# Experts' second product: both halves of the weights side by side in one product of 512 columns, and the two sums of a slot added on GpSimd

## The chip, the cores and the metric

The kernel runs on one core of one Trainium2 chip. The time is the device time of one execution in microseconds. Three runs before the change lie between 5408.88 and 5410.27, median 5409.32.

## The reference

Three layers follow each other over 8 x 3072 = 24576 tokens of 256 values.

```python
attn = np.maximum(z @ z.T / S, 0.0) ** 2      # per batch, S = 3072
x = u * (attn @ v)
e_idx = np.argmax(x @ w_gate, axis=1)         # one of 8 experts for each token
out = np.zeros((N, D))
for e in range(E):
    mask = e_idx == e
    h = np.maximum(x[mask] @ w1[e], 0.0)      # w1[e]: 256 x 1024
    ye = h @ w2[e]                            # w2[e]: 1024 x 256
    out[mask] = gate_w[mask, None] * eom[mask, e, None] * ye
h = out @ w_in                                # 256 x 2048
result = (h / (1.0 + np.exp(-h))) @ w_out     # 2048 x 256
```

The change touches `h @ w2[e]`, the experts' second product.

## The kernel before

To reach the reference's precision every float32 operand is split in two parts that TensorE takes: a high part (`hi`, a copy rounded to the type of the product) and the rest (`lo`). A product is then the sum of three: high with high, low with high and high with low. `split` makes the two parts, the high one on ScalarE (L107) or VectorE (L109), the rest on VectorE as a subtraction of two SBUF operands (L110).

The work goes through three stages: attention, which also sends each token's row to a place in DRAM that belongs to its expert; the experts; the last layer. In the experts' stage the tokens stand in 103 slots of 256 rows (`NSLOT`), each with one expert. A slot is four steps (`NSUB`), each for 256 of the 1024 hidden values, so there are 412 steps k. The instruction streams are written out by hand: each engine runs its instructions in the order in which the loop over k issues them. Step k issues:

- `s1(k+2)`: the first product of step k+2, 12 products of 256 columns (L739), into a bank of PSUM; then ScalarE writes `h`, the high part of the rectified result (L743), and VectorE writes `l`, the rest, from PSUM and `h` (L744);
- `v1(k)`: the second product of step k, 12 products of 256 columns (L760). For each half h of the slot's 256 rows and each i of two blocks of hidden values there are three: `h` with the weights' low part, `l` with the high part, `h` with the high part. All add to one PSUM bank `acc` of 2 x 256 columns, which stays open for the slot's four steps;
- in a slot's first step `x1_prep(t+1)`: VectorE transposes the gathered rows of the next slot (`xt`, L721), ScalarE writes their high part `x1h`, VectorE the rest `x1l`; s1 of the next slot's first step reads them, and is issued two steps later; then `x_gather(t+3)` on GpSimd's queue (L703);
- in a slot's last step `y_store(t)`: ScalarE copies `acc` to `yt` in SBUF (L766), and an indirect DMA from GpSimd's queue sends the rows to DRAM (L767);
- `w_ahead(k)`: splits of coming steps' weights (`w0b` for the first product, five steps ahead, `w1b` for the second, three ahead), ScalarE and VectorE in turn, and gathers of raw weights for a slot two later (L681);
- from step 96 on some instructions of `w_last`, which convert the last layer's weights (L789 to L801, tiles `wraw` and `wt`), mostly on VectorE.

So VectorE's order in a step is l, then xt and x1l in a slot's first step, then w0b, w1b and the conversion; ScalarE's is h, then x1h or yt, then w0b and w1b. PSUM has two pools of four banks, `ps_s` for the first products and `ps_a` for `acc`. `yt` has two buffers in SBUF. The last slot's sums go to `ylast`, and are stored after the last layer has begun.

Of the kernel before, what the change touches and what calls it, by code (L numbers as in the profile page):

```python
# [8 lines left out]
F32 = mybir.dt.float32  # L9
# [4 lines left out]
AF = mybir.ActivationFunctionType  # L14
ALU = mybir.AluOpType
# [11 lines left out]
B, S, D, DQK = 8, 3072, 256, 64  # L27
# [3 lines left out]
P = 128  # L31
# [8 lines left out]
NSLOT = NT // T + E - 1  # L40
# [15 lines left out]
def fused_kernel(ctx: ExitStack, tc: tile.TileContext, uT, v, zT, wg, w1, w2, w_in, w_out, out):  # L56
    nc = tc.nc
    ve, sc, pe, gp_, sy = nc.vector, nc.scalar, nc.tensor, nc.gpsimd, nc.sync
# [9 lines left out]
    ps_a = ctx.enter_context(tc.tile_pool(name="ps_a", bufs=4, space=bass.MemoryType.PSUM))  # L68
# [36 lines left out]
    def split(hi, lo, src, eng="v"):  # L105
        if eng == "a":
            sc.activation(hi, src, AF.Copy)  # L107
        else:
            ve.tensor_copy(hi, src)  # L109
        return ve.tensor_sub(lo, src, hi.bitcast(F32))  # L110

    beat = []
# [449 lines left out]
    for b in range(1, B):  # L562
        first = (b - 1) * NCH * NJ
# [100 lines left out]
    mp = p1.enter_context(tc.tile_pool(name="mp", bufs=2, reuse_waits="tile"))  # L664
# [5 lines left out]
    XG, X1H, X1L, H1, L1, ACC1, WB = {}, {}, {}, {}, {}, {}, {}  # L670
# [3 lines left out]
    def table(idx, t):  # L674
        return idx[0 if t < NEARLY else 1][:, t:t + 1]
# [11 lines left out]
    def w_split(k, which):  # L687
        if k >= NS1:
            return
        t, fp = divmod(k, NSUB)  # L690
        if which == 0:
            src = raw1[t % 2][:, :, fp * 2 * P:(fp + 1) * 2 * P]
        else:
            src = raw2[t % 2][:, 2 * fp:2 * fp + 2, :]
        w = fp_.tile([P, 2, 2, 2 * P], F32R, name=f"w{which}b", tag=f"w{which}b", bufs=4)
        beat.append(split(w[:, 0], w[:, 1], src, "a"))
        WB[which, k] = w

    def x_gather(t):
# [47 lines left out]
    def v1(k):  # L747
        t, fp = divmod(k, NSUB)
        if fp == 0:
            ACC1[t] = ps_a.tile([P, 2, D], F32, name="acc1", tag="acc")  # L750
        acc = ACC1[t]
        hi, lo = H1.pop(k), L1.pop(k)
        wb = WB.pop((1, k))
        for h in range(2):
            for i in range(2):
                first = fp == 0 and i == 0 and h == 0
                ts = slice(h * P, (h + 1) * P)
                fin = fp == NSUB - 1 and i == 1
                for x, hl, end in ((hi, 1, False), (lo, 0, False), (hi, 0, fin)):
                    pe.matmul(acc[:, h, :], x[:, i, ts], wb[:, hl, i, :], start=first, stop=end,  # L760
                              skip_group_check=True)
                    first = False

    def y_store(t):
        yt = mp.tile([P, 2, D], F32, name="yt", tag="yt", bufs=2) if t < NSLOT - 1 else ylast
        sc.activation(yt, ACC1.pop(t), AF.Copy)  # L766
        gp_.indirect_dma_start(  # L767
            y_d[:, :], bass.IndirectOffsetOnAxis(ap=table(xidx, t), axis=0),
            yt.rearrange("p h d -> p (h d)"), None, bounds_check=NSLOT * P - 1, oob_is_err=False,
        )  # L770
# [141 lines left out]
    def w_ahead(k):  # L912

        for which, n in ((0, k + min(4 + k, 6)), (1, k + min(2 + k, 4))):
            while done[which] < n:
                j = done[which]
                w_split(j, which)
                if j % NSUB == NSUB - 1:
                    w_gather(j // NSUB + 2, which)
                done[which] += 1  # L920
# [29 lines left out]
    x1_prep(0)  # L950
    x_gather(3)
    w_split(0, 0)
    w_split(1, 0)
    w_split(0, 1)
    w_split(2, 0)
# [5 lines left out]
    for k in range(NS1):  # L961
        t, fp = divmod(k, NSUB)
# [4 lines left out]
        for f, a in late.get(k, []):  # L967
            if f in ON_PE:
                f(*a)
        v1(k)  # L970
        if fp == 0:
            x1_prep(t + 1)
            if t + 3 >= 4:
                x_gather(t + 3)
        if fp == NSUB - 1 and t < NSLOT - 1:
            y_store(t)
# [22 lines left out]
        if k == 72:  # L999
# [4 lines left out]
            ylast = wr.tile([P, 2, D], F32, name="ylast")  # L1004
# [9 lines left out]
    for k in range(L1K):  # L1014
        h2(k)
    y_store(NSLOT - 1)
    for k in range(L1K, LOOK):
        s2(k)
# [56 lines left out]
```

## Time and profile before

| | us |
|---|---|
| median of three runs | 5409.32 |
| the profiled execution | 5408.52 |
| its span, first to last instruction | 5406.8 |
| TensorE busy | 5350.7 |
| VectorE busy | 4439.7 |
| ScalarE busy | 2985.1 |
| GpSimd busy | 2054.7 |

The experts' stage lies between about 2113 and 3316 us of the span. The mean granted clock of TensorE over the span is 0.998 of full speed. Busy times are unions of an engine's instructions; a matmul's end is modelled, so TensorE's busy time says little of what its pace is, and the distance from one start to the next says more. "Idle before" is the time for which an engine had nothing running ahead of an instruction, and the name behind the arrow is what released it. A DMA that GpSimd issues counts as busy time of GpSimd while its descriptors are written.

### The profile page before, as it was taken

To read this page: it belongs to the slowest core of one execution; us is meant where nothing else is said; L and a number is where in the kernel's file an instruction comes from. 1 tells how busy PE (TensorE), PEld (TensorE's weight loads), DVE (VectorE), ACT (ScalarE), POOL (GpSimd) and SP (SyncE) were. 2 spreads that over 40 slices of the span, in tenths; PEclk is the share of its full clock that TensorE was granted. 3 is DMA by queue.
4 is the path that set the end of the run, shared out by engine and by line. 5 is a ranking of instruction groups with operands and counts; after the bars stand their busy time and mean duration, and the time that the engine had idled before them with its cause. 6 is when DMAs were issued, how large, how long until landed. Compare 5 with 4: busy or idle time off the path is not lost.

```text
span 5406.8 us, 102756 instructions
## 1 busy us (share of the span) xinstructions
PE 5350.7 (99%) x37448; PEld 4789.9 (89%) x37448; DVE 4439.7 (82%) x9831; ACT 2985.1 (55%) x5555; POOL 2054.7 (38%) x1961
## 2 busy tenths in 40 slices
PE   9999999999999998999999999999999999999999
PEld 8888989898989898999999999888888888888887
DVE  8888888888888887888888887777777777777776
ACT  8777777777777776666666664222222222222222
POOL 0444333333333334443333345333333333333331
PEclk9999999999999999999999999999999999999999
DMA  7111111111111101252222221000000000000000
GB/s 271 43 45 43 43 42 48 47 39 46 39 47 39 39 25 67 77 188 92 85 88 88 89 84 38 25 25 25 25 25 24 27 26 24 25 24 25 25 25 21
DMA packets 142428, 287.06 MB, mean 53 GB/s; under 512 B 55904, under 2 KB 55904, under 8 KB 135520
## 3 DMA queue, kind: packets, MB, share of 16 engines
q0 software_dynamic: 95152, 156.97, 9.4%
q1 hardware_dynamic: 46768, 123.51, 6.6%
q8 instruction: 296, 4.85, 0.4%
q14 instruction: 212, 1.74, 0.1%
HBM read 338.44 MB, written 104.33 MB: 82 GB/s over the span
## 4 chain that ended last, share of the span: by engine, by line
PE 77%; DVE 13%; ACT 5%; issue 4%; POOL 0%; DMA 0%; SPq 0%; POOLq 0%; DVEq 0%; ACTq 0%
PE s L877 19%; PE acc L222 14%; PE s L739 10%; PE acc L760 10%; PE acc L901 6%; PE acc L899 6%; PE acc L900 6%; PE sc L222 4%; DVE lo L110 3%; DVE hi L109 2%; ACT r L245 1%; ACT a L250 1%; DVE z L296 1%; DVE l L320 1%; ACT hi L107 1%
## 5 line engine op out<-in xcount | busy, mean ns | idle before, releaser
L463 POOL DMA_INDIRECT x_d<-z,xi x768 | 783.8, 1021 | 1365.3 <-DVE lo L110 919.6
L884 ACT ACTIVATE sg<-s 128x512 f32<-128x512 f32 x768 | 459.3, 598 | 1525.4 <-PE s L877 1523.3
L833 POOL DMA_INDIRECT yg<-y_d,yi x768 | 807.6, 1052 | 1217.7 <-DVE l L110 1147.2
L222 PE MATMUL acc<-hi,vl 64*128 64x512 f32 x4608 | 1236.9, 391 | 7.5 <-DVE z L282 5.3
L222 PE MATMUL acc<-lo,vh 64*128 64x512 f32 x4608 | 1225.9, 388 | 0.6 <-DVE lo L110 0.5
L222 PE MATMUL acc<-hi,vh 64*128 64x512 f32 x4608 | 1223.6, 387 | 0.0
L877 PE MATMUL s<-yh,wi 128*128 128x512 f32 x3072 | 1070.3, 389 | 0.0
L110 DVE TENSOR_TENSOR lo<-a,hi 128x512 fp32r<-128x512 f32 x1152 | 794.7, 690 | 107.3 <-ACT hi L107 77.7
L885 DVE TENSOR_TENSOR sg<-s,sg 128x512 f32<-128x512 f32 x768 | 530.7, 691 | 418.1 <-ACT sg L884 407.2
L250 ACT ACTIVATE a<-r 128x512 f32<-128x512 f32 x1152 | 707.4, 629 | 142.6 <-DVE lo L110 141.8
L222 PEld LDWEIGHTS acc<-hi,vl 64*128 64x128 f32 x4608 | 730.0, 184 | 50.7 <-DVE z L282 9.4
L222 PEld LDWEIGHTS acc<-hi,vh 64*128 64x128 f32 x4608 | 730.2, 184 | 39.1
L222 PEld LDWEIGHTS acc<-lo,vh 64*128 64x128 f32 x4608 | 728.7, 184 | 38.0 <-DVE lo L110 1.6
L245 ACT ACTIVATE r<-sc 128x512 f32<-128x512 f32 x1152 | 622.4, 592 | 211.7 <-PE sc L222 211.3
L877 PEld LDWEIGHTS s<-yh,wi 128*128 128x128 f32 x3072 | 576.6, 188 | 119.6
L739 PE MATMUL s<-x1h,w0b 128*128 128x256 f32 x3296 | 663.6, 284 | 10.3 <-DVE w0b L110 10.3
L760 PE MATMUL acc<-w1b,h 128*128 128x256 f32 x3296 | 660.8, 283 | 0.0
L877 PE MATMUL s<-yl,wi 128*128 128x512 f32 x1536 | 597.6, 389 | 0.0
L901 PE MATMUL acc<-h,wo 128*128 128x512 f32 x1536 | 597.5, 389 | 0.0
L899 PE MATMUL acc<-h,wo 128*128 128x512 f32 x1536 | 597.5, 389 | 0.0
L900 PE MATMUL acc<-l,wo 128*128 128x512 f32 x1536 | 597.5, 389 | 0.0
L739 PEld LDWEIGHTS s<-x1h,w0b 128*128 128x128 f32 x3296 | 545.0, 192 | 10.9 <-DVE w0b L110 10.0
(210 smaller groups left out, 10443.4 us busy)
## 6 DMA issues: line engine op xcount, KB each, us to landing
x_d<-zero SPq DMA_DIRECT2D x25, 1024.0 KB, 12.5
vr<-in_v_dram SPq DMA_DIRECT2D x48, 512.0 KB, 4.5
ut<-in_uT_dram SPq DMA_DIRECT2D x48, 512.0 KB, 3.6
out_dram<-ot SPq DMA_DIRECT2D x48, 512.0 KB, 2.6
zz<-in_zT_dram SPq DMA_DIRECT2D x96, 128.0 KB, 5.0
x_d<-z,xi POOLq DMA_INDIRECT x768, 2.2
yg<-y_d,yi POOLq DMA_INDIRECT x768, 2.5
wraw<-in_w_in_dram SPq DMA_DIRECT2D x16, 256.0 KB, 2.7
```

The lines of the kernel that those rows point to most:

```text
L110: return ve.tensor_sub(lo, src, hi.bitcast(F32))
L222: pe.matmul(out, x[h][h * HP:(h + 1) * HP, w], y[h][h * HP:(h + 1) * HP, m], start=start, stop=stop, skip_group_check=True)
L245: sc.activation(r, SC[k], AF.Relu, scale=1.0 / S)
L250: sc.activation(a, RR.pop(k), AF.Square)
L463: i = gp_.indirect_dma_start(x_u, bass.IndirectOffsetOnAxis(ap=xi4[:, q * NB + c:q * NB + c + 1], axis=0), Z[q][:, c, :], None, bounds_che ...
L739: pe.matmul(ps[:, i, :], wb[:, hl, dc, fs], xx[:, dc, :], start=(n == 0), stop=(n == 5))
L760: pe.matmul(acc[:, h, :], x[:, i, ts], wb[:, hl, i, :], start=first, stop=end, skip_group_check=True)
L833: i = gp_.indirect_dma_start(YG[m][:, c, :], None, y_u[:n, :], bass.IndirectOffsetOnAxis(ap=yi4[:, m * NB + c:m * NB + c + 1], axis=0), bo ...
L877: pe.matmul(ps, wi[:, hl, dc, fs], xx[:, dc, :], start=(n == 0), stop=(n == 5))
L899: pe.matmul(acc, wo[:, 1, fc, es], hi, start=(fc == 0), stop=False)
L900: pe.matmul(acc, wo[:, 0, fc, es], lo, start=False, stop=False)
L901: pe.matmul(acc, wo[:, 0, fc, es], hi, start=False, stop=(fc == FC2 - 1))
```

## The change

The weights of the second product are laid out so that, for each i, the high and the low part stand side by side, 2 x 256 columns. One product of 512 columns takes `h` against both; a second one of 256 columns takes `l` against the high part. A half of the slot's rows now has a PSUM bank of its own, whose first 256 columns hold the sum of high with high and low with high, and whose other 256 hold high with low. At the slot's end ScalarE copies both banks to one SBUF tile, GpSimd adds its two halves, and its queue sends the rows as before. That tile has one buffer of twice the size. In the last slot ScalarE copies one half of each bank and VectorE adds the other.

```diff
-        beat.append(split(w[:, 0], w[:, 1], src, "a"))
+        parts = (w[:, 0], w[:, 1]) if which == 0 else (w[:, :, 0, :], w[:, :, 1, :])
+        beat.append(split(*parts, src, "a"))
...
-            ACC1[t] = ps_a.tile([P, 2, D], F32, name="acc1", tag="acc")
+            ACC1[t] = [ps_a.tile([P, 2, D], F32, name="acc1", tag="acc") for h in range(2)]
...
-                first = fp == 0 and i == 0 and h == 0
+                first = fp == 0 and i == 0
                 ts = slice(h * P, (h + 1) * P)
                 fin = fp == NSUB - 1 and i == 1
-                for x, hl, end in ((hi, 1, False), (lo, 0, False), (hi, 0, fin)):
-                    pe.matmul(acc[:, h, :], x[:, i, ts], wb[:, hl, i, :], start=first, stop=end,
-                              skip_group_check=True)
-                    first = False
+                pe.matmul(acc[h], hi[:, i, ts], wb[:, i].rearrange("p a b -> p (a b)"), start=first, stop=False,
+                          skip_group_check=True)
+                pe.matmul(acc[h][:, 0, :], lo[:, i, ts], wb[:, i, 0, :], start=False, stop=fin,
+                          skip_group_check=True)
...
-        yt = mp.tile([P, 2, D], F32, name="yt", tag="yt", bufs=2) if t < NSLOT - 1 else ylast
-        sc.activation(yt, ACC1.pop(t), AF.Copy)
+        if t < NSLOT - 1:
+            both = mp.tile([P, 2, 2, D], F32, name="yt", tag="yt", bufs=1)
+            for h, acc in enumerate(ACC1.pop(t)):
+                sc.activation(both[:, :, h, :], acc, AF.Copy)
+            yt = both[:, 0]
+            gp_.tensor_tensor(yt, yt, both[:, 1], ALU.add)
+        else:
+            yt = ylast
+            for h, acc in enumerate(ACC1.pop(t)):
+                sc.activation(yt[:, h, :], acc[:, 0, :], AF.Copy)
+                ve.tensor_add(yt[:, h, :], acc[:, 1, :], yt[:, h, :])
```

## Rows read from the trace of the kernel before

**Rows 1.** The page: busy time of each engine, share of the span, instructions.
```profile
PE 5350.7 (99%) x37448; PEld 4789.9 (89%) x37448; DVE 4439.7 (82%) x9831; ACT 2985.1 (55%) x5555; POOL 2054.7 (38%) x1961
```

**Rows 2.** The page: the chain that ended last, share of the span by line.
```profile
PE s L877 19%; PE acc L222 14%; PE s L739 10%; PE acc L760 10%; PE acc L901 6%; PE acc L899 6%; PE acc L900 6%; PE sc L222 4%; DVE lo L110 3%; DVE hi L109 2%; ACT r L245 1%; ACT a L250 1%; DVE z L296 1%; DVE l L320 1%; ACT hi L107 1%
```

**Rows 3.** Table of stretches: us, busy us (instructions) per engine, granted clock, DMA, GB/s.
```profile
2550.00:2650.00 100.00, 100.00 (x831) 99.53 (x830) 87.78 (x165) 66.49 (x127) 39.18 (x36) 1.00 0.30 101
```

**Rows 4.** The chain in order of time: start us, us, what; both product stages.
```profile
2948.20 1.44 PE acc L760 x12
...
2961.35 1.63 PE s L739 x12
...
3322.49 1.36 PE s L877 x6
```

**Rows 5.** Timeline of ScalarE, one slot: start us, us, engine, line, operation, [idle before].
```profile
2955.63 0.60 ACT L766 ACTIVATE yt<-acc 128x512 f32<-128x512 f32 x1 [0.78 <-PE acc L760]
2956.12 0.62 ACT L107 ACTIVATE w0b<-raw 128x512 fp32r<-128x512 f32 x1
...
2967.33 0.60 ACT L766 ACTIVATE yt<-acc 128x512 f32<-128x512 f32 x1 [0.78 <-PE acc L760]
```

**Rows 6.** Timeline of VectorE in the same slot.
```profile
2955.89 0.69 DVE L744 SCALAR_TENSOR_TENSOR l<-s,h 128x512 fp32r<-128x512 f32 x1
2956.78 0.69 DVE L110 TENSOR_TENSOR w0b<-raw,w0b 128x512 fp32r<-128x512 f32 x1 [0.20 <-ACT w0b L107]
...
2960.65 0.69 DVE L110 TENSOR_TENSOR x1l<-xt,x1h 128x512 fp32r<-128x512 f32 x1 [0.70 <-ACT x1h L107]
```

**Rows 7.** Timelines of ScalarE and VectorE in a slot three later.
```profile
2990.37 0.60 ACT L766 ACTIVATE yt<-acc 128x512 f32<-128x512 f32 x1 [0.78 <-PE acc L760]
...
2994.73 0.69 DVE L110 TENSOR_TENSOR x1l<-xt,x1h 128x512 fp32r<-128x512 f32 x1 [0.70 <-ACT x1h L107]
```

**Rows 8.** Timeline of TensorE where the experts' stage and the last layer meet.
```profile
3311.02 0.39 PE L877 MATMUL s<-yh,wi 128*128 128x512 f32 x1
...
3311.25 0.28 PE L760 MATMUL acc<-w1b,h 128*128 128x256 f32 x1
...
3311.36 0.28 PE L760 MATMUL acc<-w1b,l 128*128 128x256 f32 x1
```

**Rows 9.** Waits between 2400 and 3316 us: us in total, times, longest.
```profile
ACT yt L766 <- PE acc L760: 61.3, 79, 0.8
```

**Rows 10.** Timeline of GpSimd at four places.
```profile
2951.11 0.99 POOL L681 DMA_INDIRECT raw<-in_w_dram,widx  x1 [3.84 <-DVE w1b L110]
...
2956.51 1.03 POOL L767 DMA_INDIRECT y_d<-yt,xidx  x1 [0.33 <-ACT yt L766]
...
2608.82 1.03 POOL L767 DMA_INDIRECT y_d<-yt,xidx  x1 [0.30 <-ACT w0b L107]
...
3278.55 1.50 POOL L833 DMA_INDIRECT yg<-y_d,yi  x1 [0.30 <-issue]
```

**Rows 11.** Timeline of VectorE at three of these places.
```profile
2951.09 0.68 DVE L744 SCALAR_TENSOR_TENSOR l<-s,h 128x512 fp32r<-128x512 f32 x1
...
2608.78 0.76 DVE L110 TENSOR_TENSOR w0b<-raw,w0b 128x512 fp32r<-128x512 f32 x1 [0.33 <-ACT w0b L107]
...
3278.50 0.68 DVE L110 TENSOR_TENSOR w0b<-raw,w0b 128x512 fp32r<-128x512 f32 x1
```

**Rows 12.** GpSimd's groups by line: operation, names, shapes, count | busy us, mean ns | idle.
```profile
L126 POOL MEMSET zero<- 128x512 f32 x1 | 0.5, 514 | 0.0
...
masks.py:199 POOL TENSOR_SCALAR_AFFINE_SELECT ident<-ident 128x128 f32<-128x128 f32 x1 | 0.3, 286 | 0.1
...
masks.py:197 POOL MEMSET ident<- 128x128 f32 x1 | 0.2, 204 | 0.3 <-POOLq L1062 0.3
```

**Rows 13.** Timelines of ScalarE and GpSimd near the stage's end.
```profile
3269.32 0.60 ACT L766 ACTIVATE yt<-acc 128x512 f32<-128x512 f32 x1 [0.78 <-PE acc L760]
...
3282.34 1.03 POOL L767 DMA_INDIRECT y_d<-yt,xidx  x1 [2.29 <-ACT w0b L107]
```

## The prediction, made before the change was run

> **What bounds the kernel now.** I read the page first: TensorE is busy for 99% of the span [rows 1], and the chain of work that ended last runs mostly over its lines, with 10% each on the experts' two products, s1 (L739) and v1 (L760) [rows 2]. Then the table of stretches: in the middle of the experts' stage TensorE is busy all 100 us of 100, VectorE 87.8, ScalarE 66.5, GpSimd 39.2, at the full granted clock (1.00, the 2.4 GHz level) [rows 3]. So the stage looks like TensorE's alone. The chain in order of time says how near it is to something else: twelve products of 256 columns take 1.44 us, 120 ns each, one piece for s1 and one for v1, but here and there an s1 takes 1.63 [rows 4]. The timelines tell what that is. A slot is four steps, 8 x 1.44 = 11.52 us. When its last v1 ends, ScalarE copies the sums (yt, 2955.63), then splits the next w0b (2956.12) [rows 5]; VectorE has been waiting for that split and starts its own half at 2956.78, then goes through w1b, the conversion of the last layer's weights, l, the transpose, and at last x1l, which ends at 2960.65 + 0.69 = 2961.34 [rows 6]. The s1 of 2961.35 in the same chain needs x1l, and is one of the long ones. From yt's start to x1l's end, which I call D, is 5.71 us here, and the next yt comes 11.70 after this one, 0.18 over 11.52 [rows 5, 6]. In a slot without conversion work on the way D is 2994.73 + 0.69 - 2990.37 = 5.05 [rows 7]. I read D for all 101 slots that have both rows: 25 are at 5.05, 22 at 5.71, 44 lie between (mean 5.40), 10 above (mean 5.88); the mean is 5.43. Below about 5.53 the next yt comes 11.52 later, and above it by as much later as D is over 5.53. So there are two bounds that nearly touch: TensorE, and a chain ScalarE - VectorE - ScalarE - VectorE that starts at the end of each slot's v1 and ends in x1l. The excess over 11.52 is now 11 x 0.03 + 22 x 0.18 + 10 x 0.35 = 7.8 us in all.
>
> **Products.** Per step 12 products of 256 columns become 4 of 512 and 4 of 256; the columns are 3072 before and after. What is saved is what a product costs beside its columns. Six products of 512 take 1.36 us, 226.7 ns each [rows 4]; against 120 for 256, that is 106.7 per 256 columns and 13.3 per product. Where the two widths already meet, at the stage's end, a 512 is followed after 0.23 and a 256 after 0.11 [rows 8], so they add up. After: 4 x (226.7 + 120) = 1387 against 1440, 53 ns per step and 412 x 0.0533 = 22.0 us in all; per slot 0.213, so TensorE's slot is 11.307. The Trainium skill (TensorE: Matmul & The Clock Gate, Back-to-back issue gap) puts a product's own cost at 2.5 ns beside its columns, which would make the gain 412 x 4 x 2.5 ns = 4 us; the trace has 13.3, so the row decides.
>
> x1l's limit moves too: two v1 lie inside it, so it falls from 5.53 to 5.53 - 2 x 0.053 = 5.42. If D stayed as it is, the stage would stall 11 x 0.14 + 22 x 0.29 + 10 x 0.46 = 12.5 us in place of 7.8, and the change would bring 22.0 - 12.5 + 7.8 = 17.3 us.
>
> **The second copy.** ScalarE copies two banks, 0.49 us from start to start each [rows 5]. The first needs only half h = 0, whose products end 0.69 us before v1 does, and ScalarE idles 0.78 before yt today, in 79 slots of the middle stretch 61.3 us [rows 9]. So the first copy lies in that idle time and the second starts where yt starts now: cost nothing. If that cover were gone (the first copy held until all of v1 is done), D would grow by 0.49 in each slot, some 50 us.
>
> **The add on GpSimd.** This is the part that decides. The send now starts 2956.51, 0.88 after yt's start [rows 10]; in its place stands an add of 512 elements that reads two operands in SBUF, ahead of the send in the same queue. What waits behind it there are the gathers of x and of raw weights, which the steps of two slots later read; those 23 us cover them, and if they didn't each slot would lose up to the add's length. What is not covered is VectorE. The trace has no add on GpSimd, but it shows what a GpSimd read of SBUF and a VectorE instruction with two inputs in SBUF do to each other. A send whose start falls 0.05 us into such a VectorE instruction takes 1.50 in place of 0.99 or so (3278.55, in the w0b of 3278.50); one that falls into an l, whose one input is in PSUM, takes 0.99 (2951.11, in the l of 2951.09) [rows 10, 11]. Where GpSimd is first by a hair, it is VectorE that is longer, 0.76 in place of 0.69 (2608.78) [rows 11]. One waits until the other's reads are over; they don't share. A send reads an index column only, hence the 0.07. An add reads for all its length, and it begins at 0.88, just ahead of VectorE's w0b at 2956.78, 1.15 after yt [rows 6], which has two inputs in SBUF. The l before w0b (2955.89 to 2956.58) has one and holds nothing up.
>
> So w0b, and with it x1l, comes later by d = 0.88 + T - 1.15, T being the add's length. Bounds for T from GpSimd's own rows: a memset of 512 takes 0.514, one of 128 takes 0.204, so 0.81 ns an element; two reads through one path at that rate, and the fixed 0.10, give 0.93; a select of 128, which reads as well as writes, takes 0.286, 0.08 more than the memset of 128, and two such reads of 512 on top of the memset give 0.514 + 8 x 0.082 = 1.17 [rows 12]. The low end is 0.51, an add as fast as a memset. The two that count reads are nearer to what an add does; I take their middle, 1.05, and d = 0.78. The Trainium skill (GPSIMD Engine Reference, Performance versus the Vector engine) gives 4497 ns for an add of 2048; a quarter, 1.12, would be an estimate that makes d 0.85 and the sum below 7 us larger; no row here shows an add.
>
> The same sum with d = 0.78: every slot is now over the limit, 101 x (5.43 + 0.78 - 5.42) = 80 us of stall in place of 7.8, less 22.0 of products: +50 us. VectorE's own time per slot, 87.8% of 11.6 = 10.2 plus 0.8 held and 0.7 in which it waits for x1h [rows 3, 6], stays under the new slot of 12.1, so no third bound opens.
>
> **Smaller parts.** yt has one buffer in place of two. Where GpSimd's queue is full its send starts late: 3282.34 for the yt of 3269.32, 13.0 us [rows 13]. With one buffer the next slot's first copy, due 11.5 - 0.65 = 10.9 after that yt, waits for it: 2 us, and 1.05 more for each add that has gone into the queue in that stretch, some five, so up to 8. In the other crowded stretch, where the scatters end, the latest send is 10.4 late: up to 5. I price it at nothing to 13 us, 3 taken, since longer slots give GpSimd time. In the same 12 slots the add comes too late to stand before w0b, and may hold an instruction that has slack: -5 of the 50. The new order of w1b's halves leaves the count of elements as it is: nothing. The last slot's halves go over ScalarE and VectorE, and behind its send in GpSimd's queue stand gathers that wait for the last layer's first products, which hide it: nothing, and without that cover a microsecond, once.
>
> The sum: 5408.5 of the profiled execution (span 5406.8; 0.8 under the median of 5409.3) + 50 + 3 - 5 = 5456.5. Against the median, 5456 or 5457; I give 5456.
>
> **Rivals.** (a) The intended gain: VectorE isn't held, because the add lies elsewhere or its reads let others in; D stays, 17 us less 0 to 13 for the buffer: about 5395, faster. Against it stand the 1.50 and the 0.76. It decides at d under 0.1. (b) A short hold: T near 0.51, d about 0.24, the stall 12.5 grows to some 28, and gain and loss meet: 5407, no change. The memset speaks for it, but it reads nothing. (c) The first copy waits for all of v1, so 0.49 comes on top: +50 + 49, about 5506. Against it: each copy reads a tile of its own. (d) The change doesn't do what it says: 512 beside 256 costs what it costs now, v1 stays 1.44. Two of a slot's four v1 lie in the chain from x1l to the next yt, so half the 22 us is lost from the sum: 101 x (5.43 + 0.78 - 5.53) - 7.8 - 2 = +59, 5467. Against it: [rows 8]. The Trainium skill (SBUF — State Buffer, Who interferes with whom) has whoever starts first keep the shared pair for its whole instruction; the trace agrees as far as a send's 0.99 and 1.50 show it, and it would give the forecast, not (a) or (b).
>
> **How the numbers follow.** Forecast 0.71, (a) 0.10, (b) 0.10, (c) 0.05, (d) 0.04. About 0.2%, 11 us, is what a measurement can tell from no change. Slower by more: forecast, (c), (d), 0.80; within: (b), 0.10; faster: (a), 0.10. The range goes from d = 0.3 (+3, with the buffer at nothing; 5410) to T = 1.17 with a start 0.15 later and the buffer at 13 (d = 1.05, +77 + 13; 5500). Below it lie (a) and (b), above it (c).
>
> **What would show it.** Right: v1's piece at 1.39; yt copies twice per slot, the first 0.65 before v1 ends; an add of about 1.05 us at 0.9; the w0b of VectorE behind it starting, or lasting, about 0.8 later; s1 pieces of about 2.2 us in nearly every slot, and TensorE waiting for x1l. Wrong: a w0b at 1.15 with 0.69 beside a running add; a slot of 11.3; or x1l late for another reason, ScalarE still copying when w0b is due.

## The result, and the profile after

The changed kernel takes 5489.84 us (median of four runs, 5489.15 to 5490.72) against 5409.80 for the kernel before: the ratio is 1.0148, interval 1.0135 to 1.0160, or 80 us more. The profiled execution took 5489.78, its span is 5487.8. The forecast was 5456, slower, with a range from 5410 to 5500.

The page, busy time of each engine (before: [rows 1]), and the stretch in the middle of the experts' stage (before: [rows 3]; the columns are the same):

```profile
PE 5377.3 (98%) x35800; PEld 4716.9 (86%) x35800; DVE 4536.5 (83%) x9833; ACT 3042.6 (55%) x5658; POOL 2196.3 (40%) x2063
```

```profile
2550.00:2650.00 100.00, 96.75 (x656) 87.73 (x656) 90.58 (x160) 65.30 (x123) 48.40 (x42) 1.00 0.21 63
```

TensorE was busy 100 us of 100 and now has gaps, at the same full clock. VectorE is busier than before although it got no work in this stretch. The whole 80 us lie in the experts' stage: from its first s1 to the end of its last v1 it takes 1284.5 us (2112.1 to 3396.7) where it took 1202.7.

One slot, read across the engines; a slot without conversion work on the way, like that of [rows 7]. GpSimd, ScalarE and VectorE from the timeline of the changed kernel (start, us, engine, line, operation, idle before):

```profile
2231.59 1.26 ACT L771 ACTIVATE yt<-acc 128x512 f32<-128x512 f32 x2
2232.75 0.63 ACT L107 ACTIVATE w0b<-raw 128x512 fp32r<-128x512 f32 x1
2232.94 1.29 POOL L773 TENSOR_TENSOR yt<-yt 128x512 f32<-128x512 f32 x1 [0.28 <-ACT yt L771]
...
2233.41 1.37 DVE L110 TENSOR_TENSOR w0b<-raw,w0b 128x512 fp32r<-128x512 f32 x1 [1.01 <-ACT w0b L107]
...
2234.51 1.19 POOL L779 DMA_INDIRECT y_d<-yt,xidx  x1 [0.28 <-POOL yt L773]
2234.71 0.68 DVE L110 TENSOR_TENSOR w1b<-raw,w1b 128x512 fp32r<-128x512 f32 x1
...
2237.30 0.69 DVE L110 TENSOR_TENSOR x1l<-xt,x1h 128x512 fp32r<-128x512 f32 x1 [0.70 <-ACT x1h L107]
```

The add runs from 2232.94 to 2234.23. VectorE's w0b begins inside it, lasts 1.37 in place of 0.69 [rows 6], and ends 0.55 after the add. The w1b behind it, beside the send, takes 0.68 as always. Counted from the second copy's start, 2232.26 (0.67 into the pair of the first row), x1l ends after 5.73, and in the same kind of slot it was 5.05 before [rows 7]: the 0.68 that w0b is longer. Where a gather stands ahead of the add on GpSimd's queue, the add is later and w0b with it. A slot in the middle of the stage:

```profile
2952.03 1.26 ACT L771 ACTIVATE yt<-acc 128x512 f32<-128x512 f32 x2
2952.61 1.20 POOL L681 DMA_INDIRECT raw<-in_w_dram,widx  x1 [3.39 <-DVE w0b L110]
2953.84 1.29 POOL L773 TENSOR_TENSOR yt<-yt 128x512 f32<-128x512 f32 x1
2953.85 1.85 DVE L110 TENSOR_TENSOR w0b<-raw,w0b 128x512 fp32r<-128x512 f32 x1
...
2959.08 0.69 DVE L110 TENSOR_TENSOR x1l<-xt,x1h 128x512 fp32r<-128x512 f32 x1 [0.69 <-ACT x1h L107]
2959.10 0.38 PE L741 MATMUL s<-x1h,w0b 128*128 128x256 f32 x1 [0.74 <-ACT x1h L107]
2959.83 0.38 PE L741 MATMUL s<-x1l,w0b 128*128 128x256 f32 x1 [0.34 <-DVE x1l L110]
```

TensorE stands still twice, 0.74 and 0.34: for x1h, then for x1l. That stall is most of what the change costs (in this slot the add is late and D is 7.07, one of the longer ones). Over the stage it shows in the groups by line between 2400 and 3100 us (count | busy us, mean ns of one | idle before) and in the waits between 2400 and 3316 us (us in total, times, longest; before, the wait of the weight load for x1l came to 2.0 us):

```profile
L110 DVE TENSOR_TENSOR w0b<-raw,w0b 128x512 fp32r<-128x512 f32 x228 | 202.1, 887 | 26.8 <-ACT w0b L107 26.1
L773 POOL TENSOR_TENSOR yt<-yt 128x512 f32<-128x512 f32 x57 | 74.0, 1298 | 8.1 <-ACT yt L771 6.4
```

```profile
PEld s L741 <- DVE x1l L110: 38.0, 74, 0.5
...
PEld s L741 <- ACT x1h L107: 24.6, 43, 1.6
PE s L741 <- DVE x1l L110: 23.0, 70, 0.3
```

There are four w0b to one add, so a mean of 887 in place of 684 is 0.81 us more for the one that meets it.

**The sum of the stage**, read slot by slot. The mean of D over the 101 slots goes from 5.43 to 6.29. The next yt comes 5.95 after x1l's end wherever TensorE had to wait for it, and the shortest slot that TensorE alone allows is 11.41 (before 11.52). So the stalls through x1l, D + 5.95 - 11.41 summed over the slots where it is positive, are 85 us; by the same sum they were 6 before. What slots take beyond that is 18 us, nearly all in slots 2, 4, 11 to 14, 97 and 98; before it was 4. Products give back 0.11 in each of 103 slots, 11 us. Together: +79 + 14 - 11 = +82, and the stage is 1284.5 - 1202.7 = 81.8 longer.

### The profile page after: what moved, and what is told of

It is laid out like the page before. It is cut to its first block, busy times and chain, and to the rows that moved or that the text cites. A ratio compares the mean times of both kernels' runs of the same rounds, so it can differ in the third digit from the quotient of the medians.

```text
span 5487.8 us, 99671 instructions
## 1 busy us (share of the span) xinstructions
PE 5377.3 (98%) x35800; PEld 4716.9 (86%) x35800; DVE 4536.5 (83%) x9833; ACT 3042.6 (55%) x5658; POOL 2196.3 (40%) x2063
## 5 line engine op out<-in xcount | busy, mean ns | idle before, releaser
L110 DVE TENSOR_TENSOR lo<-a,hi 128x512 fp32r<-128x512 f32 x1152 | 794.8, 690 | 106.7 <-ACT hi L107 77.0
L762 PE MATMUL acc<-w1b,h 128*128 128x512 f32 x1648 | 604.7, 400 | 0.0
## 6 DMA issues: line engine op xcount, KB each, us to landing
x_d<-zero SPq DMA_DIRECT2D x25, 1024.0 KB, 12.5
```

Source lines behind the costliest of these rows:

```text
L762: pe.matmul(acc[h], hi[:, i, ts], wb[:, i].rearrange("p a b -> p (a b)"), start=first, stop=False, skip_group_check=True)
```

## Experiments

Each is compared with the kernel before on the same chip. That kernel took 5423.34 on the chip of the first four below, 5410.40 on that of the next four and 5410.11 on that of the last three; so times go by the ratio, not from one chip to another.

### The changed kernel without its add

```diff
             yt = both[:, 0]
-            gp_.tensor_tensor(yt, yt, both[:, 1], ALU.add)
```

> The changed kernel without GpSimd's add (the product of the high part with the weights' low part is left out of the rows that are sent). Theory H (the add holds VectorE's instructions that have two SBUF inputs, because it reads SBUF all the while): w0b behind yt is back at 0.69 us from 1.55 and 1.85, D (second yt copy to the end of x1l) is back at a mean of 5.4 from 6.3, and the products' 1.41 in place of 1.44 becomes visible: -12 us of products, +3 of stalls at the shorter slot, +5 to +12 for the single buffer: about 5405 us. Rival Q (the add's time in GpSimd's queue delays sends and gathers): also about 5405, so this run doesn't part H from Q. Rival C (the second ScalarE copy or the single buffer is the cause): still about 5480.

Measured: 5423.31, ratio 1.0001 (0.9991 to 1.0011): no difference from before. VectorE's w0b is back, in its group by line between 2400 and 3100 us:

```profile
L110 DVE TENSOR_TENSOR w0b<-raw,w0b 128x512 fp32r<-128x512 f32 x243 | 166.4, 685 | 35.0 <-ACT w0b L107 30.8 <-ACT yt L771 2.7 <-issue 1.2
```

D is 5.44. So all that the add costs is 80 us, and the two copies, the banks and the new weights' order bring no stall in a common slot. (About 5 us less than before were expected.) The products' 11 us are there (slots of 11.41), and are spent: 5 us because the limit moved under the same D (11.4 us of stall through x1l where there were 6.3), and 7 in the crowded slots (10.9 where there were 3.7), where one buffer holds the copies. The forecast had the first of the two (12.5 against 7.8) and 3 for the second.

### Memsets in the add's place

```diff
-            gp_.tensor_tensor(yt, yt, both[:, 1], ALU.add)
+            for _ in range(3):
+                gp_.memset(both[:, 1], 0.0)
```

> In place of the add, three memsets of 512 elements on GpSimd, on the half of the tile that is not sent: as long in the queue (3 x 0.46 us from start to start, about 1.4 in all, against 1.30), but they read nothing (the product of the high part with the weights' low part is left out of the rows that are sent). Theory H: w0b stays at 0.69, D at about 5.4, and only the crowded stretches lose to the single buffer, some 20 us: 5415 to 5425 us. Rival Q: GpSimd is busy for as long as before, so still about 5480. Rival W (writes hold VectorE as reads do): w0b at 1.4 or more, also about 5480; the length of w0b parts W from Q.

Measured: 5430.88, ratio 1.0015 (1.0005 to 1.0024). GpSimd is busy in front of the send for longer than with the add, but only writes. Groups by line, 2400 to 3100 us:

```profile
L110 DVE TENSOR_TENSOR w0b<-raw,w0b 128x512 fp32r<-128x512 f32 x244 | 166.8, 684 | 35.6 <-ACT w0b L107 35.2
L774 POOL MEMSET yt<- 128x512 f32 x183 | 96.8, 529 | 21.5 <-issue 13.7
```

1.59 us of memsets in each slot, and w0b stays 0.684, D 5.43. Over the whole trace 207 of VectorE's subtractions of two SBUF operands (L110) run beside a memset, and none takes more than 0.70. So it is the add's reads that hold w0b, not GpSimd's being busy and not the send's coming later. The 7.5 us that remain are in the crowded slots (18.7 us there, as in the changed kernel): that is what a longer queue costs with one buffer. The Trainium skill (SBUF — State Buffer, Who interferes with whom) says that a VectorE instruction with two inputs in SBUF is at odds with a GpSimd instruction that reads SBUF, and not with one that only writes; the trace agrees on both, 1.37 and 0.684.

### The kernel before with one buffer

```diff
-        yt = mp.tile([P, 2, D], F32, name="yt", tag="yt", bufs=2) if t < NSLOT - 1 else ylast
+        yt = mp.tile([P, 2, D], F32, name="yt", tag="yt", bufs=1) if t < NSLOT - 1 else ylast
```

> The kernel before with one buffer for yt in place of two, nothing else. If the single buffer holds ScalarE's copy where sends are late, the slots after those whose send starts more than about 8 us after yt (10.4, 13.0 and two others today) wait: 3 + 3 + 5, some 8 to 12 us in all, 5418 to 5422. If the buffer costs nothing: 5410.

Measured: 5429.39, ratio 1.0013 (1.0003 to 1.0023), +6. ScalarE's copies near the stage's end, from its timeline:

```profile
3271.04 0.60 ACT L766 ACTIVATE yt<-acc 128x512 f32<-128x512 f32 x1 [0.37 <-ACT h L743]
3283.14 0.60 ACT L766 ACTIVATE yt<-acc 128x512 f32<-128x512 f32 x1 [1.14 <-DMA y_d<-yt,xidx]
3296.45 0.60 ACT L766 ACTIVATE yt<-acc 128x512 f32<-128x512 f32 x1 [1.05 <-DMA y_d<-yt,xidx]
```

In five slots (14, 95, 96, 98 and 99) the copy starts 0.40 to 0.95 behind v1's end, in place of 0.09; in 14, 98 and 99 the trace names the send of the slot before as what released it. The mechanism is the one priced in the forecast, twice as dear as the 3 taken and inside 0 to 13.

### The kernel before with an add

```diff
         sc.activation(yt, ACC1.pop(t), AF.Copy)
+        if t < NSLOT - 1:
+            gp_.tensor_tensor(yt, yt, yt, ALU.add)
```

> The kernel before with one instruction more: GpSimd adds yt to itself before the send (so the experts' rows are doubled). Two buffers, one copy, products of 256 columns as before. Theory H: the add takes 1.3 us, w0b behind yt grows to 1.4 or more, D by 0.7 to 0.9, and with the products at their old pace a slot takes D + 5.99: 6.25 + 5.99 = 12.24 in place of 11.62, +63 us, and a little for GpSimd's full queue: about 5475. If the products or their layout are part of the loss, less: 5440 or below. If the add costs nothing beside the rest: 5410.

Measured: 5474.70, ratio 1.0097 (1.0080 to 1.0114), +51. Groups by line, 2400 to 3100 us:

```profile
L110 DVE TENSOR_TENSOR w0b<-raw,w0b 128x512 fp32r<-128x512 f32 x232 | 188.9, 814 | 33.1 <-ACT w0b L107 32.9 <-issue 0.2
...
L768 POOL TENSOR_TENSOR yt<-yt 128x512 f32<-128x512 f32 x58 | 60.4, 1041 | 11.5 <-ACT yt L766 10.2
```

An add with nothing else of the change slows the kernel by 51 us. It is less than the 65 expected, and the add itself is shorter here: with one tile for both operands it takes 1.04, with two different ones 1.30. w0b grows by 4 x (814 - 684) = 0.52 in each slot, and D to 6.00.

### The add on VectorE, with the store

```diff
-            for h, acc in enumerate(ACC1.pop(t)):
-                sc.activation(both[:, :, h, :], acc, AF.Copy)
-            yt = both[:, 0]
-            gp_.tensor_tensor(yt, yt, both[:, 1], ALU.add)
...
+        yt = mp.tile([P, 2, D], F32, name="yt", tag="yt", bufs=2) if t < NSLOT - 1 else ylast
...
+            sc.activation(yt[:, h, :], acc[:, 0, :], AF.Copy)
...
+        for h, acc in enumerate(accs):
+            ve.tensor_add(yt[:, h, :], acc[:, 1, :], yt[:, h, :])
```

> The changed products, but all slots end as the last one does: ScalarE copies 256 columns of each bank, VectorE adds the other 256 from PSUM, right there, two buffers. VectorE has 2 x 0.35 us more from start to start in each slot, between l and w0b, where it waits 0.73 on the mean today; w0b's first half comes 0.11 sooner, since the copies are shorter. Theory: D grows by 0 to 0.5, 0.15 on the mean; slots over the limit of 5.47 stall by some 20 us in all, the products give 12: about 5410, between 5402 and 5425. If VectorE's added time counts in full: +0.7 x 101 - 12, 5465.

Measured: 5417.42, ratio 1.0012 (1.0002 to 1.0022), +7. VectorE's timeline in one slot:

```profile
2958.02 0.68 DVE L746 SCALAR_TENSOR_TENSOR l<-s,h 128x512 fp32r<-128x512 f32 x1
2958.62 0.74 DVE L778 TENSOR_TENSOR yt<-acc,yt 128x256 f32<-128x256 f32 x2
2959.28 0.68 DVE L110 TENSOR_TENSOR w0b<-raw,w0b 128x512 fp32r<-128x512 f32 x1
```

The two halves' adds take 0.74 on VectorE, 0.66 from start to start, and stand just ahead of w0b, but part of that falls into its old wait for ScalarE: D is 5.61, 0.18 more. So in D the work itself, on the busier engine, costs a fifth of what the hold costs (0.18 for 0.86). 73 us of the 80 are gone; the second buffer and the shorter copies have a part in that, which this run doesn't separate.

### The add in VectorE's gap

VectorE waits 0.70 in each slot between xt and x1l [rows 6]. Here the adds go there (`between` is the two adds and the send of the slot before); they read PSUM and one SBUF tile.

```diff
-        split(hi, lo, xt, "a")
+        sc.activation(hi, xt, AF.Copy)
+        if between:
+            between()
+        ve.tensor_sub(lo, xt, hi.bitcast(F32))
```

> As the run with VectorE's add, but the two adds stand between xt and x1l of the next step, where VectorE waits 0.70 us for x1h today. They take about 0.77 there, and w0b's first half comes 0.11 sooner. Theory (the chain from yt to x1l is what the stage can lose on): D stays at 5.4, stalls at 8 to 11 us as before, the products give 12: about 5398, between 5394 and 5404. If VectorE's total time is the bound instead: no better than the run with the adds before w0b.

Measured: 5398.30, ratio 0.9977 (0.9967 to 0.9986), -12. D is 5.26, slots 11.51. D falls by 0.17, since the copies ahead of w0b are shorter. The adds cost nothing that shows, and what stands is the gain of the products.

### The kernel before, x1l one step sooner

```diff
-        if fp == 0:
+        if k == 0 or t == NSLOT - 2 and fp == 0:
             x1_prep(t + 1)
...
+        if fp == NSUB - 1:
+            if t < NSLOT - 3:
+                x1_prep(t + 2)
+            if t < NSLOT - 1:
+                y_store(t)
```

> The kernel before with x1_prep of each slot issued one step sooner, ahead of yt, so that x1l no longer follows yt on VectorE and ScalarE. Theory (the excess over 11.52 per slot comes from that chain alone): the 8 us of stalls go, s1 takes 1.44 nearly everywhere: about 5402, between 5400 and 5405. If VectorE's total time is the cause of the stalls: no change, 5410.

Measured: 5407.37, ratio 0.9994 (0.9984 to 1.0003), -3: not told from no change. ScalarE's timeline shows a wait that the move brought with it:

```profile
2952.41 0.63 ACT L107 ACTIVATE x1h<-xt 128x512 fp32r<-128x512 f32 x1 [1.67 <-DVE xt L721]
2952.95 0.58 ACT L766 ACTIVATE yt<-acc 128x512 f32<-128x512 f32 x1
2953.42 0.62 ACT L107 ACTIVATE w0b<-raw 128x512 fp32r<-128x512 f32 x1
```

x1h now waits for xt ahead of yt in ScalarE's order, and yt, which starts 1.17 behind v1's end (median of the slots), takes w0b along. Of 101 slots 42 are 11.52 and most others lie within 0.36 of that; one (98) is 16.92, and its rows are sent only 15.2 after its copy's start. What makes that slot so long was not looked into.

### The gap, and x1l one step sooner

The edits of the last two together, on the changed products: `x1_prep(t + 2, lambda: y_add(t))` in a slot's last step, behind the two copies.

> VectorE's adds between xt and x1l, and x1_prep one step sooner, right behind the copies: x1l now has a whole step, 2.8 us, to spare, and the slot should be TensorE's alone, 11.40. Theory: products 12 and stalls 8 to 10 gained: about 5389, between 5386 and 5394. Rival: VectorE's time per slot, 10.2 plus 0.8 of adds, and its waits for yt make a new bound: 5398 or more.

Measured: 5390.84, ratio 0.9964 (0.9950 to 0.9979), -20. VectorE and ScalarE in one slot:

```profile
2956.49 0.70 DVE L725 STREAM_TRANSPOSE xt<-xg 128x512 f32<-128x512 f32 x1
2956.62 0.39 ACT L778 ACTIVATE yt<-acc 128x256 f32<-128x256 f32 x1 [0.33 <-PE acc L769]
2957.12 0.72 DVE L783 TENSOR_TENSOR yt<-acc,yt 128x256 f32<-128x256 f32 x2
2957.23 0.63 ACT L731 ACTIVATE x1h<-xt 128x512 fp32r<-128x512 f32 x1 [0.23 <-DVE xt L725]
...
2957.90 0.69 DVE L734 TENSOR_TENSOR x1l<-xt,x1h 128x512 fp32r<-128x512 f32 x1
```

The adds fill the time in which x1h is made, without a gap on either side. Nearly every slot is 11.41: the stage runs at the products' pace.

### The change, x1l one step sooner

The same move of `x1_prep` in the changed kernel, with its add on GpSimd.

> The changed kernel, add on GpSimd and all, with x1_prep of each slot one step sooner, ahead of yt, so that x1l doesn't follow the held w0b. If the chain yt - w0b - x1l is the only way by which the hold reaches TensorE, the slot falls back to 11.4 to 11.5 and the crowded stretches keep 20 us: 5409 - 12 + 15, about 5415. If VectorE's total is a bound just behind it (10.2 busy, 0.7 waiting for x1h, 1.3 held: 12.2 a slot), nearly nothing comes back: 5460 to 5475.

Measured: 5501.17, ratio 1.0171 (1.0154 to 1.0188): 11 us above the changed kernel, outside both expectations. The timeline of one slot:

```profile
2946.39 0.70 DVE L723 STREAM_TRANSPOSE xt<-xg 128x512 f32<-128x512 f32 x1
...
2947.12 0.63 ACT L107 ACTIVATE x1h<-xt 128x512 fp32r<-128x512 f32 x1 [3.56 <-DVE xt L723]
2947.66 1.07 ACT L771 ACTIVATE yt<-acc 128x512 f32<-128x512 f32 x2
2947.79 0.69 DVE L110 TENSOR_TENSOR x1l<-xt,x1h 128x512 fp32r<-128x512 f32 x1 [0.70 <-ACT x1h L107]
...
2948.61 0.63 ACT L107 ACTIVATE w0b<-raw 128x512 fp32r<-128x512 f32 x1
...
2949.28 1.38 DVE L110 TENSOR_TENSOR w0b<-raw,w0b 128x512 fp32r<-128x512 f32 x1 [0.80 <-ACT w0b L107]
...
2950.80 0.36 PE L741 MATMUL s<-x1h,w0b 128*128 128x256 f32 x1 [0.81 <-DVE w0b L110]
```

x1l is no longer late, but TensorE now waits 0.81 for w0b itself. The order has closed a loop that TensorE isn't in: VectorE's xt, then on ScalarE x1h, two copies and w0b's high part, then VectorE's w0b. In each slot VectorE waits 0.70 and 0.80 in it and is held 0.69 by the add. Its busy time in the stretch from 2550 to 2650 us, with the hold in it, is 87.57 of 100; of a slot of 12.5 that is 10.95, and with 1.50 of waits 12.45. VectorE's round is full and sets the slot. The round shown bears it out: xt starts at 2946.39 and again at 2958.90, and between them VectorE's timeline has no other wait. So this run doesn't show what the add costs beside a relaxed x1l, since the edit brought a wait of its own; it does show that the hold takes VectorE's time wherever x1l stands.

### The change with two buffers

```diff
-            both = mp.tile([P, 2, 2, D], F32, name="yt", tag="yt", bufs=1)
+            both = mp.tile([P, 2, 2, D], F32, name="yt", tag="yt", bufs=2)
```

(`h1` and `l1` have three buffers in place of four, to make room.)

> The changed kernel with two buffers for the tile that both sums are copied to; to make room h and l have three buffers in place of four. Theory: the copies of the crowded slots no longer wait, so most of the 20 us over the rule D + 5.95 come back: 5470 to 5478. If the single buffer isn't what these slots lose on, no change: 5490.

Measured: 5481.62, ratio 1.0134 (1.0117 to 1.0150): 8 us under the changed kernel. Copies of slot 12, from ScalarE's timeline, first of the changed kernel, then of this one:

```profile
2282.79 1.09 ACT L771 ACTIVATE yt<-acc 128x512 f32<-128x512 f32 x2 [4.56 <-DMA y_d<-yt,xidx]
```

```profile
2281.14 1.26 ACT L771 ACTIVATE yt<-acc 128x512 f32<-128x512 f32 x2
```

With one buffer the copies of slot 12 waited for the send of slot 11. With two they wait for nothing but v1, slots 11 and 12 are at 11.41 (15.71 and 13.93 in the changed kernel), and the time beyond the stalls through x1l falls from 18 to 5 us; the rest of the stage stalls 4 us more (89 for 85). So the one buffer costs about 8, less than the 12 to 20 that were expected back. (Three buffers for h and l in place of four are part of this run; whether they cost anything was not tried.)

### The gap, sooner, and products of one width together

The version with the gap and x1l sooner, and in each v1 the four products of 512 columns ahead of the four of 256.

```diff
-        for h in range(2):
-            for i in range(2):
...
+        for lo_part in range(2):
+            for h in range(2):
+                for i in range(2):
...
+                    if not lo_part:
```

> VectorE's adds between xt and x1l and x1_prep one step sooner, as before, and v1's four products of 512 columns ahead of its four of 256, in place of one after the other. A pair of 512 and 256 measures 353 ns in the changed kernel where the two alone make 226.7 + 120 = 346.7. If the price lies in each change of width, v1 goes from 1.41 to 1.39: -8 to -10 us against the alternating order, about 5381. If it lies in the products of 512 themselves in this place, no change: 5390.

Measured: 5382.87, ratio 0.9952 (0.9936 to 0.9969): 8 us under the kernel it differs from, and 27 under the kernel before, the fastest here. TensorE's timeline, v1 of one step, first in the changed kernel, then here:

```profile
2953.93 0.40 PE L762 MATMUL acc<-w1b,h 128*128 128x512 f32 x1
2954.16 0.28 PE L764 MATMUL acc<-w1b,l 128*128 128x256 f32 x1
2954.28 0.40 PE L762 MATMUL acc<-w1b,h 128*128 128x512 f32 x1
...
2955.34 0.28 PE L741 MATMUL s<-x1h,w0b 128*128 128x256 f32 x1
```

```profile
2953.62 1.09 PE L768 MATMUL acc<-w1b,h 128*128 128x512 f32 x4
2954.55 0.63 PE L771 MATMUL acc<-w1b,l 128*128 128x256 f32 x4
2955.02 0.28 PE L746 MATMUL s<-x1h,w0b 128*128 128x256 f32 x1
```

From 2953.93 to 2955.34 are 1.41, four pairs of 0.353; 226.7 + 120 would be 0.347. Grouped it is 1.40 by these rows. By the slots, of which 4 steps are 11.33 in place of 11.41, a step is 20 ns shorter. The same products, in another order: so the order is worth 20 ns a step, 8 us. That the price lies in each change of width (two in place of eight, 20 / 6 = 3.3 ns each) is not shown, and the rows speak against it as the whole: over the undisturbed steps v1 falls from 1415 to 1401 ns, the other 5 ns are in s1, and the four products of 512 that now follow each other still take 0.93 here, 232.5 ns each and not 226.7. Why was not looked into.

## Why the prediction came out as it did

Its course was right and its sum 33 us short (+47 forecast, +80 measured). Step by step:

- **Products.** Mis-sized by half: 22.0 us forecast at 53 ns a step, 11 measured at 27 (slots of 11.41 for 11.52). The row it rests on, [rows 8], shows 0.23 and 0.11 to two digits, and what is missing is 6.7 ns in a pair; so "they add up" was said from a row that couldn't show it. Rival (d), which gave the whole of it up, was off by as much the other way. Grouping the widths gives 20 of the missing 27 ns a step back, which the last experiment shows. That costs the sum 11 us, and the limit's move is 5.53 to 5.46 in place of 5.42: 4 us the other way, a stall less by 101 x 0.04.
- **The second copy.** Right: the first starts 0.66 before the second (forecast 0.65), the second starts 0.04 behind v1's end in 97 of the 101 slots, and without the add the kernel has D at 5.44.
- **The hold.** Right in kind, near in size. Without the add there is no hold; with GpSimd just as busy but writing only, there is none either. The two sizes that went into d were both off and by luck nearly made up for each other: the add takes 1.30, not 1.05 (it is above the bound of 1.17 that was worked out from the memset and the select), and starts at 0.68, not 0.88, since it begins 0.09 after the copies' end where the send began 0.28 after it [rows 5, 10]. It ends at 1.97 in the first slot shown, forecast 1.93, and at 2.4 in the second, behind a gather. w0b is longer by 0.75 on the mean of the 101 slots, forecast d 0.78. D grew by 0.86: another 0.09 lies between w0b's end and x1l's start, where the conversion work stands (2.96 for 2.87), and 0.03 in x1l itself (0.73 for 0.69). The Trainium skill (GPSIMD Engine Reference, Performance versus the Vector engine) would have given an estimate of 1.12 for the add, which the 1.30 in this trace exceeds as well. Two words in the evidence for the hold need care. The "sends" of 3278.55 and 2951.11 are gathers (L833, L681), which does not change what they show. And the row that is called "GpSimd first by a hair" has GpSimd's start 0.04 after VectorE's (2608.82, 2608.78), so who is first can't be read from the starts alone; the changed kernel has stronger cases of that, in the last section.
- **The stall.** 101 slots over the limit were forecast, 80 us; 96 are, 85 us. The pace behind x1l is near the forecast, 5.95 from its end to the next yt for 11.307 - 5.42 = 5.89.
- **Crowded slots.** Mis-sized. The forecast took 3 for the buffer and took 5 off for adds that come late. The adds do come late (4 to 8 us behind the copies in slots 95 to 98, and w0b is 0.69 there), but that relief is in the measured mean of D already, so the 5 belong to the 85 and not beside them; and beyond the stalls through x1l the slots at both ends are 14 us longer than before. Two buffers take 12 of that away, 8 in the whole time. "Longer slots give GpSimd time" failed: in slots 11 and 12 the add starts 9.0 us behind the copies, with gathers and the attention's scatters ahead of it in the queue.
- **VectorE's own time.** The sentence "no third bound opens" held for the changed kernel, but not by much: in the version with x1l sooner VectorE's round of 12.45 is the bound.

In the sum, 11 for the products, 85 - 80 for the stalls, 14 for the crowded slots where -2 was forecast, and 2 for the smaller stall before (6.3 for 7.8) make 34, the 82 of the stage less 48; the medians differ by 33. Rival (a) fell on the w0b of 1.37, and (b) on the add's 1.30; the memset that spoke for it holds nothing. (c) fell on the first copy's 0.66.

## What to carry to other kernels

An engine's free time is no place for work if that work's operands go through what the critical engine needs: with the add on GpSimd, 40% busy, the change is 80 us slower than the kernel before; with it on VectorE, 88% busy in this stage, 7 slower; and in VectorE's own wait for ScalarE 12 faster, which is the products' gain. (The last two also have two buffers, worth about 8.) Before moving work, list which instructions with two SBUF inputs of VectorE will stand beside it, and whether one of them begins a chain. And where products of two widths share a step, it is worth trying those of one width together (8 us here); a price read from two neighbours at two digits doesn't tell.

## What the runs showed of the hardware that was not expected

- A GpSimd add of 128x512 float32 takes 1.30 us with two different operands and 1.04 with the same tile as both (57 and 58 instructions, means 1.298 and 1.041). A memset of that size in the same place takes 0.53.
- A w0b that starts inside a GpSimd add ends 0.55 to 0.57 after it, 0.68 being its own length; so it is in all 81 such slots of the changed kernel, and why it does not need all of that again was not looked into.
- Nor does the earlier start decide. Behind a gather or a scatter, 15 of the 102 adds start 0.05 to 0.62 after a VectorE instruction with two SBUF inputs by the profile, and it is VectorE that waits: it ends 0.55 or 0.56 after the add, and the add stays at 1.27 to 1.32. One of them, from the timelines of GpSimd and VectorE:

```profile
2707.07 1.00 POOL L681 DMA_INDIRECT raw<-in_w_dram,widx  x1 [4.21 <-DVE l L746]
2707.48 2.47 DVE L110 TENSOR_TENSOR w0b<-raw,w0b 128x512 fp32r<-128x512 f32 x1 [0.61 <-ACT w0b L107]
2708.09 1.30 POOL L773 TENSOR_TENSOR yt<-yt 128x512 f32<-128x512 f32 x1
```

In the kernel before, no w0b, w1b or x1l that starts inside a gather or a send takes more than 0.71. Here too one of the two waits for the other; but the rule quoted beside the rivals, that whoever starts first keeps the pair, does not fit these starts. Starts on GpSimd are rough in the profile, and whether the add's reads begin before its start was not tested.

- Two products of 512 and 256 columns in turn take 0.353 us a pair, some 7 ns over 226.7 (512 in the last layer) and 120 (256 before the change). Sorted by width a step is 20 ns shorter, 15 in v1 and 5 in s1, though the 512s in a row take 232.5 each.
